# Windowed attention into a folded gated FFN on one core: first q, k loaded first and uncast, the weight fold by columns and then by rows, PSUM copies on either engine, a later believed DMA landing

## The chip, the cores and the metric

The kernel runs on one core of a Trainium2 chip. The metric is the device time of one execution in microseconds (us); the profile's span is about 2 us shorter. PE is the matmul engine, and PEld its weight load. DVE and ACT are the vector and scalar engines. POOL issues the loads that cast fp32 to bf16, and SP issues stores and DMA transposes. "Granted clock" (PEclk) is the share of full PE clock that the throttle grants. A run is called slow when it is over 1.5% above the fastest of the same kernel.

## The reference, cut to what matters

```python
# attention: q, k, v are (4, 8, 768, 64) fp32
scores = q @ k.T / 8          # keep the first 4 keys ("sink") and a causal window of 128
x = softmax(scores) @ v       # -> (3072, 512)
# feed-forward part
a = x @ w1; b = x @ w2        # 512 -> 1024 each
out = ((a * b) @ w3) @ w_out  # 1024 -> 1024 -> 512, fp32
```

Both kernels fold `w3 @ w_out` at the start into one 1024x512 matrix, `w3o`, so that the last two products become one for each token block. Four batches, 0 to 3, follow one another. Each has attention, "gate" products (with w1 and w2) and a "projection" (with w3o), in two halves of 384 tokens.

## The kernel before: the parts that matter

The program does not fix its instruction order by hand. It makes a list of operations with dependencies and modelled durations, and a list scheduler inside it picks, engine by engine, what it believes can start soonest. The order is frozen when the kernel is built.

```python
# POOL issues its casting loads in this order:
LOADS = """wo0 ident w3-1 wo1 w3-2 w3-3 wo2 k0-0-0 q0-0-0 tri k0-0-4 q0-0-4 w3-4 pick v0-0 v0-1 v0-2
    w3-5 w3-6 w3-7 w0 w1 k0-1-0 q0-1-0 v0-3 v0-4 v0-5 w2 w3
    b1-0 b1-1 b1-2 b1-3 b1-4 b1-5"""        # b1-n: k, q, v block n of batch 1
# (cut) batches 2 and 3: q, k are transposed by DMA from SP; the loads alternate k, q, v
for kb in range(NB):
    for s, n, src in ((0, "k", kN), (1, "q", qN)):
        got[n, b, kb] = load_nat(src, k if n == "k" else q, b, kb, fold_done)
        ...
        tp_of[s, kb] = Op(SP, TUS, dmt, [got[n, b, kb]] + war, base)
        tp_of[s, kb].turn = TUS
    got["v", b, kb] = load_v(b, kb)
# (cut) fold: one row block i of w3 at a time: 8 transposes, DVE copy, products, ACT copy
cpy = Op(DVE, dve_us(KFF * P, 2), lambda f=t3c, x=boxc: f(op=x), [a2], pr, frees=[(a, "mm")])
...
# (cut) x is transposed on PE for batches 0 and 1, by DMA for 2 and 3
if b < 2:
# (cut) what the scheduler picks on an engine: shortest wait, then priority
key = (0.0 if wait < 0.05 else wait, o.prio, o.serial)
# (cut) the landing belief
if hasattr(o, "turn"):                       # DMA transposes and stores
    busy = dma["at"] > start + 0.6
    dma["at"] = max(dma["at"], start + 0.6) + o.turn
    o.done = start + 0.6 + o.turn * (2 if busy else 1) + 1.3
if hasattr(o, "dma"):                        # loads
    dma["at"] = max(dma["at"], start + us + (0.1 if e == POOL else 0.6)) + o.dma
    o.done = dma["at"] + LAND
```

Two of PE's products are markers. `mm<-vN,sel` is the first that needs a batch's v, and only its first block ("v2-0" is that of batch 2). `mm<-qkT,ksbd`, the sink scores, is the first that needs a batch's transposed q and k.

The softmax here doesn't subtract the row's maximum and nothing guards it: scores larger than these inputs give would overflow.

## Time and profile before

| what | before | view |
|---|---|---|
| time | 215.36 us, median of 3 runs (214.5 to 229.22, the highest a slow run) | runs |
| span profiled, a fast run | 213.0 us | page |
| PE busy | 92% (DVE 51%, ACT 47%) | page, busy time |
| PE's longest wait | 4.9 us, before batch 2's sink scores | waits of PE |
| granted clock just after it | 0.57 | windows |

These lines are from the page of the kernel before. They are PE's line of busy time, three rows of the 40 equal slices of 5.3 us (busy share and granted clock in tenths), and the summary by engine of the chain that ended last.

```profile
PE 196.4 (92%) x1880; PEld 122.4 (57%) x1880; DVE 108.2 (51%) x249; ACT 100.1 (47%) x172; POOL 71.1 (33%) x93
PE   8899699969879999559999999999999999999994
PEclk9999999999999999958999999999999999999999
DMA  7999999999999999999999453210163030030033
PE 65%; DMA 25%; POOL 7%; issue 2%; ACT 0%; SPq 0%; POOLq 0%; ACTq 0%
```

PE is the only engine near its limit, and it is dense from slice 19 on. Whatever can be won lies in the first 100 us, where DMA is at 9 tenths. The dips of PE's row there are times in which the work in the frozen order waited for data.

The next lines are the waits of PE in the kernel before: engine, tile and line, what released it, total us, times, longest.

```profile
PE mm L427 <- DMA qkT<-big: 4.9, 1, 4.9
PE mm L407 <- DMA vN<-in_v_dram: 3.3, 3, 2.0
```

The next lines are from PE's timeline (start, us, instruction, count, and in brackets the idle time just before it with its releaser).

```profile
87.72 0.28 PE L538 MATMUL av<-vN,am 128*128 128x65 bf16 x4
92.91 0.62 PE L427 MATMUL mm<-qkT,ksbd 128*32 128x512 bf16 x4 [4.90 <-DMA qkT<-big]
```

The last one is the stretch after that wait in the windows view: stretch, us, then busy time of PE, PEld, DVE, ACT and POOL with counts, granted clock, DMA share, GB/s.

```profile
92.91:98.75 5.84, 5.84 (x35) 2.97 (x37) 2.26 (x4) 3.17 (x5) 1.64 (x2) 0.57 1.73 201
```

So the hole costs twice: 4.9 us idle, and then 5.8 us at little more than half speed. The last of batch 2's twelve DMA transposes of q, k landed at 92.66 us, by the trace's landing records, and PE went on at 92.91 us.

### The profile page before, as it was taken

The numbers are of one execution on the slowest core, as the hardware profiler recorded it, in microseconds if no ns is written. First come the engines' busy times: TensorE is split into PE (matmuls) and PEld (weight loads), VectorE is DVE, ScalarE is ACT, GpSimd is POOL, SyncE is SP. The second block draws the span as 40 slices with busy tenths as digits, with TensorE's granted clock in tenths as the row PEclk, the third lists the DMA queues.
The fourth block names the chain that finished last, engine by engine and source line by source line (L and its number), as shares of the span: only waits on it lengthen the run. The fifth ranks groups of instructions, "written<-read, shape, count | busy, mean of one in ns | idle before, by whom it ended". The sixth has DMA issues, their size and how long they took to land.

```text
span 213.0 us, 4649 instructions
## 1 busy us (share of the span) xinstructions
PE 196.4 (92%) x1880; PEld 122.4 (57%) x1880; DVE 108.2 (51%) x249; ACT 100.1 (47%) x172; POOL 71.1 (33%) x93
## 2 busy tenths in 40 slices
PE   8899699969879999559999999999999999999994
PEld 8797465536645665335665655566555556555542
DVE  3533766565986986316786444768504404314300
ACT  3135662757137772145874237786153243233232
POOL 7856763869999354732600000000000000000000
PEclk9999999999999999958999999999999999999999
DMA  7999999999999999999999453210163030030033
GB/s 140 181 194 184 199 196 177 192 160 155 151 147 131 120 144 131 155 238 131 155 153 118 116 133 83 94 51 3 34 182 82 0 148 0 3 148 0 2 148 148
DMA packets 98437, 26.25 MB, mean 123 GB/s; under 512 B 88944, under 2 KB 94320, under 8 KB 98416
## 3 DMA queue, kind: packets, MB, share of 16 engines
q0 software_dynamic: 74944, 14.42, 89.5%
q1 hardware_dynamic: 23472, 11.54, 25.9%
q8 instruction: 14, 0.23, 0.5%
q14 instruction: 7, 0.06, 0.1%
HBM read 29.36 MB, written 6.29 MB: 167 GB/s over the span
## 4 chain that ended last, share of the span: by engine, by line
PE 65%; DMA 25%; POOL 7%; issue 2%; ACT 0%; SPq 0%; POOLq 0%; ACTq 0%
PE mm L618 35%; PE mm L648 19%; DMA vN<-in_v_dram 8%; PE av L538 5%; DMA early<-in_k_dram 5%; DMA w_sb<-in_moe_w_dram 5%; PE sc L469 4%; DMA big<-in_moe_w_dram 4%; DMA qkT<-big 3%; POOL near L153 3%; POOL big L153 2%; POOL vN L153 1%; PE mm L574 1%; PE mm L427 1%; PE mm L407 0%
## 5 line engine op out<-in xcount | busy, mean ns | idle before, releaser
L618 PE MATMUL mm<-xT,w_sb 128*128 128x384 bf16 x512 | 91.6, 329 | 0.1
L618 PEld LDWEIGHTS <-w_sb 128*128 128x128 bf16 x512 | 48.0, 99 | 35.0 <-issue 4.4
L633 DVE TENSOR_TENSOR ab<-a_sb,mm 128x384 bf16<-128x384 f32 x64 | 35.3, 553 | 52.7 <-PE mm L618 48.2
L625 ACT COPY a_sb<-mm 128x384 f32<-128x384 f32 x64 | 30.6, 479 | 38.4 <-PE mm L618 21.9
L480 ACT ACTIVATE ex<-sc 128x768 bf16<-128x768 f32 (+2 forms) x52 | 44.1, 897 | 6.9 <-PE sc L469 6.7
L648 PE MATMUL mm<-w3o,ab 128*128 128x512 bf16 (+1 forms) x200 | 43.6, 370 | 0.0
L486 DVE TENSOR_TENSOR am<-ex,maskt 128x768 bf16<-128x768 bf16 (+2 forms) x52 | 30.0, 594 | 3.1 <-ACT ex L480 3.1
L648 PEld LDWEIGHTS <-ab 128*128 128x128 bf16 x200 | 19.3, 98 | 20.4 <-issue 0.2
L655 ACT COPY o_sb<-mm 128x512 f32<-128x512 f32 (+1 forms) x25 | 14.2, 568 | 34.6 <-PE mm L648 34.5
L153 POOL DMA_DIRECT2D vN<-in_v_dram x24 | 21.3, 888 | 11.6 <-DMA big<-in_k_dram 7.0
L538 PEld LDWEIGHTS <-am 128*128 128x128 bf16 x352 | 17.0, 97 | 3.2 <-issue 0.2
L538 PE MATMUL av<-vN,am 128*128 128x65 bf16 x352 | 18.8, 193 | 0.0
L553 DVE TENSOR_TENSOR xs<-av,rec 128x384 bf16<-128x384 f32 x32 | 17.7, 552 | 0.5
L300 PE MATMUL mm<-big,w3t 128*128 128x128 bf16 (+2 forms) x128 | 15.6, 273 | 0.1
L469 PE MATMUL sc<-qkT 64*128 64x256 bf16 (+1 forms) x248 | 14.6, 245 | 0.0
L304 ACT CAST w3o<-mm 128x128 bf16<-128x128 f32 (+2 forms) x16 | 6.0, 372 | 16.9 <-PE mm L300 16.8
L153 POOL DMA_DIRECT2D big<-in_q_dram x12 | 10.6, 882 | 6.7 <-DMA vN<-in_v_dram 6.6
L538 PE MATMUL av<-vsb,es 128*128 128x130 bf16 x64 | 12.8, 219 | 0.0
L153 POOL DMA_DIRECT2D big<-in_k_dram x12 | 10.5, 879 | 4.9 <-DMA big<-in_q_dram 3.1
L469 PEld LDWEIGHTS <-qkT 64*128 64x128 bf16 x248 | 8.2, 96 | 6.2 <-issue 5.2
L300 PEld LDWEIGHTS <-w3t 128*128 128x128 bf16 x128 | 9.5, 98 | 3.7 <-issue 0.4
L548 DVE RECIPROCAL rec<-av 128x6 f32<-128x6 f32 x32 | 6.2, 192 | 9.1 <-PE av L538 9.0
(52 smaller groups left out, 122.2 us busy)
## 6 DMA issues: line engine op xcount, KB each, us to landing
out_dram<-o_sb SPq DMA_DIRECT2D x23, 256.0 KB, 2.1
vN<-in_v_dram POOLq DMA_DIRECT2D x24, 128.0 KB, 9.9
w_sb<-in_moe_w_dram POOLq DMA_DIRECT2D x8, 256.0 KB, 9.8
big<-in_moe_w_dram POOLq DMA_DIRECT2D x7, 256.0 KB, 8.2
big<-in_k_dram POOLq DMA_DIRECT2D x12, 128.0 KB, 11.1
big<-in_q_dram POOLq DMA_DIRECT2D x12, 128.0 KB, 11.4
near<-in_k_dram POOLq DMA_DIRECT2D x6, 128.0 KB, 7.2
near<-in_q_dram POOLq DMA_DIRECT2D x6, 128.0 KB, 6.6
```

Source lines behind the costliest of these rows:

```text
L153: op = Op(eng, us, lambda: (nc.gpsimd if eng == POOL else nc.sync).dma_start(out=out, in_=in_), deps)
L300: nc.tensor.matmul(po, x[1].slot["w3t"][:, j, :], wo_sb[:, j, c0:c1], start=(j == 0), stop=(j == KFF - 1))
L469: nc.tensor.matmul(sc[:, e, c * P:(c + n) * P], T[hp, r, 0, kb * P:(kb + 1) * P], T[hp, r, 1, qb * P:(qb + n) * P], start=True, stop=True)
L480: nc.scalar.activation(y[1].slot["ex"][:, :, 0:w], y[0].slot["sc", i][:, :, 0:w], ACTF.Exp, scale=scale)
L486: nc.vector.tensor_mul(y[2].slot["am"][:, :, 0:w], y[1].slot["ex"][:, :, 0:w], maskt[:, :, m0:m0 + w].to_broadcast([P, 2, w]))
L538: nc.tensor.matmul(o, lhs, rhs, start=(i == 0), stop=(i == len(todo) - 1), skip_group_check=True)
L553: nc.vector.tensor_mul(xs_first[c].slot["xs"][:, :, r * P:(r + 1) * P].rearrange("p k (e d) -> p k e d", d=D), x[0].slot["av"][:, :, :, 0: ...
L618: nc.tensor.matmul(pg[:, 0:TOK], w_sb[:, kk, dt * P:(dt + 1) * P], holder[0].slot["xT"][:, kk, :], start=(kk == 0), stop=(kk == NP - 1))
L625: nc.scalar.copy(y[1].slot["a"][:], y[0].slot["mm"][:, 0:TOK])
L633: nc.vector.tensor_mul(abh[0].slot["ab"][:, dt, :], y[1].slot["a"][:], y[2].slot["mm"][:, 0:TOK])
L648: nc.tensor.matmul(x[0].slot["mm"][:, 0:n1 - n0], abh[0].slot["ab"][:, kk, mi * P:(mi + 1) * P], w3o[:, kk, n0:n1], start=(kk == 0), stop= ...
L655: nc.scalar.copy(x[1].slot["o"][:, n0:n1], x[0].slot["mm"][:, 0:n1 - n0])
```

## The change

Its intent is to let PE start on attention sooner, to keep PE, DVE and ACT fed by placing copies on whichever is free, and to reorder loads. Its parts:

1. Batch 0's first q, k are loaded as fp32 by SP and ACT, and cast on DVE and ACT.
2. POOL's loads are reordered: batch 0's first v ahead of the fold's weights, all gate weights (`w0`..`w3`) ahead of the second half of batch 0, and the q, k loads of batches 2 and 3 ahead of all v loads of the same batch.
3. The fold handles the first three row blocks of w3 by columns into three held PSUM banks, the other five by rows.
4. Nine kinds of PSUM copies may go to ACT or DVE (`EITHER`), as the scheduler sees fit.
5. Batch 2's x is transposed on PE, not by DMA.
6. The landing belief changes: a transpose is done when the modelled DMA queue reaches it, not at most two turns after its issue; and each casting load is believed to take 2% longer.

Some smaller edits go with these: the projection's products are queued in halves of four, some set-up work is split, and the model's starting values differ.

```diff
-    LOADS = """wo0 ident w3-1 wo1 w3-2 w3-3 wo2 k0-0-0 q0-0-0 tri k0-0-4 q0-0-4 w3-4 pick v0-0 v0-1 v0-2
-        w3-5 w3-6 w3-7 w0 w1 k0-1-0 q0-1-0 v0-3 v0-4 v0-5 w2 w3
-        b1-0 b1-1 b1-2 b1-3 b1-4 b1-5"""
+    for r in range(2):
+        for n, src in enumerate((k, q)):
+            # (cut) fp32 into a home that is free until later
+            def first(r=r, n=n, src=src, i=i):
+                (nc.scalar if n else nc.sync).dma_start(out=first_home[i][...], in_=src[0, ...])
+    LOADS = """ident k0-0-4 q0-0-4 tri v0-0 pick v0-1 v0-2 w3j-0-1 wo-0-1 w3j-1-2 wo-1-2 w3j-2-4 wo-2-4
+        w3j-4-6 wo-4-6 w3j-6-8 wo-6-8 w3-3 w3-4 w3-5 w3-6 w3-7 w0 w1 w2 w3 k0-1-0 q0-1-0 v0-3 v0-4
+        v0-5 k1-0 q1-0 v1-0 (cut) k2-0 q2-0 k2-1 q2-1 k2-2 q2-2 k2-3 q2-3 k2-4 q2-4 k2-5 q2-5 v2-0 v2-1
+        v2-2 v2-3 v2-4 v2-5 (cut: batch 3 likewise)"""
@@ fold (cut)
+    for j in range(KFF):          # columns of the first KA = 3 row blocks
+        cpy = Op(EITHER, (act_us(KA * P), dve_us(KA * P, 2)), t3c, [a], ...)
+        last = Op(PE, cols(DM, KA), fm, ..., takes=["sc", "mm"] if j == 0 else [], ...)
@@ copies
-                ac = Op(ACT, act_us(TOK), acopy, [g1], 0, takes=["a"], frees=[(g1, "mm")])
+                ac = Op(EITHER, (act_us(TOK), dve_us(TOK)), acopy, [g1], 0, takes=["a"], frees=[(g1, "mm")])
@@ x transposed
-            if b < 2:
+            if b < 3:
@@ landing belief
             if hasattr(o, "turn"):
-                busy = dma["at"] > start + 0.6
                 dma["at"] = max(dma["at"], start + 0.6) + o.turn
-                o.done = start + 0.6 + o.turn * (2 if busy else 1) + 1.3
+                o.done = dma["at"] + 1.3
-            if hasattr(o, "dma"):
-                dma["at"] = max(dma["at"], start + us + (0.1 if e == POOL else 0.6)) + o.dma
+            if hasattr(o, "dma") and e == POOL:
+                dma["at"] = max(dma["at"], start + us + 0.1) + o.dma * 1.02
```

## The prediction

> **What bounds the kernel now.** The page's PE 92% busy counts waits inside matmul records. I price PE's work at the pace of dense stretches of the chain of waits (0.65 us for four 128x384 gate matmuls, 1.73 us for eight 128x512 projection matmuls), times the counts of the instruction order: about 183 of the 213.0 us span. The other 30 us, by how far PE lags behind its work (timeline of PE):
> - 13 us at 36 us (second q, k half of batch 0), 20 us at 64 us: starved by loads. The chain has 25% DMA. The last first-layer weight lands at 45.1 us, batch 1's last q at 60.3, batch 2's first v at 63.9 (PE waits for both).
> - Batch 2's twelve DMA transposes (issued 62.2 to 87.1 us) leave PE idle 4.9 us up to 92.9 us. The granted clock is then 0.57 over 92.9 to 98.8 us: about 2 us more. The Trainium skill, "TensorE: Matmul & The Clock Gate", Part 1, says an idle window of about 3.4 us halves the clock; this trace agrees.
> - Then PE is dense to 210 us; the last copy and store take 3 us.
>
> **What the change does.** PE work hardly changes: the fold keeps 64 transposes, its products become 64 of 128x512 (13.8 us; before 14 us in narrower pieces). Batch 2's xT moves from DMA to PE (24 transposes, +1.3 us). Sum: 184 us. Bytes stay. First q, k on the SP and ACT queues share the same 16 DMA engines (the skill, "DMA: Bandwidth & Descriptors", "Issuing engines are not separate DMA queues"): they win order, not bandwidth. Order changes:
> - The fold's 6 MB come after batch 0's first q, k, v; all first-layer weights before the second q, k, v half. When that lands (about 42 us, at 350 GB/s: 14.7 MB read by 45 us), 30 us of PE work stand before it in the instruction order, against 23.
> - 79 us, against 68, stand before batch 2's first scores; its q, k loads come before its v.
>
> **Where that leads.** PE lag: 9 us when the column fold's last load lands (20 us), 10 to 12 at the last gate weight, then set by batch 1's loads, still behind the same bytes: its second half lands near 60 us, with 46 us of work before it instead of 41: lag 14, not 19. Batch 2's scores are wanted near 93.5 us, ready by 80 to 92: no hole, no cold clock. 184 + 14.5 + 1.5 small stalls + 3 tail = 203 us span, plus 2.4 us from span to median time: 205.4 us.
>
> **Critical path.** About 5 us from the early order, 7 us from hole and clock, less 1.3 and small stalls. First start and engine choice (both half idle): under 2 us.
>
> **What would show it.** PE's wait on DMA qkT before batch 2's sink scores under 1.5 us; granted clock near 1.0; gate and projection lines over 58% of the chain (now 54%), DMA under 18%.
>
> **What would make it wrong.** The order is fixed from modelled times: one late load stalls everything behind it. One score bank is held during the column fold: batch 0's scores may stall. Batch 0's stores queue behind twelve transposes on SP. Then 208 to 212. If batch 1's loads come earlier: 199.
>
> 205.4 us, 8 in 10 between 200 and 211; faster by over 2%: 0.87, within 2%: 0.11, slower: 0.02.

## The result and the profile after

The changed kernel took 206.06 us in the median of 4 runs (205.12 to 211.06), against 214.93 us (214.1 to 229.22, a slow run; the other three are at most 215.36). Two more runs of the changed kernel took 206.16 and 209.72 us (slow). The ratio is 0.959, with a 95% interval of 0.9536 to 0.9644. Here and below a ratio is the mean time of one kernel's fast runs over that of the other's of the same rounds, so it is not quite the ratio of the medians.

The first profile of the changed kernel fell in a slow run (211.06 us, span 209.3). The same file was therefore run again, unedited (experiment E1), and its profile is of a fast run (206.54 us, span 204.8). That one is "the profile after" below; the slow one stands beside it where it shows something. These lines are from the page after, fast, and answer to those of before.

```profile
PE 193.1 (94%) x1778; PEld 115.8 (57%) x1778; DVE 106.5 (52%) x247; ACT 108.5 (53%) x176; POOL 73.0 (36%) x96
PE   7659999999999998999999999999999999999993
PEclk9976999999999999999999999999999999999998
DMA  6999999999999999999999933000145120030034
PE 44%; DMA 39%; POOL 12%; issue 2%; ACT 0%; DVE 0%; ACTq 0%; POOLq 0%
```

The dips of PE's row at slices 5, 9, 11 to 12 and 17 to 18 are gone. A new dip stands in slices 1 to 3, with a lower clock in slices 3 and 4, and a small one in slice 16. The page's chain now has *more* DMA than before in a faster run; this is taken up below.

The waits of PE after:

```profile
PE mm L320 <- DMA big<-in_moe_w_dram: 2.1, 3, 1.4
PE mm L461 <- DMA vN<-in_v_dram: 1.4, 3, 1.0
```

There is no wait for transposed q, k any more. The timeline shows PE passing the marker of batch 2 (last line) without idling, and a short wait for batch 2's v before it.

```profile
79.10 0.82 PE L675 MATMUL mm<-xT,w_sb 128*128 128x384 bf16 x4
80.88 0.39 PE L461 MATMUL mm<-vN,sel 128*128 128x512 bf16 x1 [0.95 <-DMA vN<-in_v_dram]
90.82 5.36 PE L675 MATMUL mm<-xT,w_sb 128*128 128x384 bf16 x32
96.11 0.40 PE L481 MATMUL mm<-qkT,ksbd 128*32 128x512 bf16 x4
```

The early stretch in the windows view, after, has the columns as above:

```profile
9.60:13.00 3.40, 1.84 (x25) 1.07 (x25) 2.68 (x7) 2.62 (x7) 3.40 (x5) 0.91 1.46 174
13.00:20.00 7.00, 5.65 (x47) 3.39 (x45) 3.22 (x9) 2.99 (x7) 3.89 (x8) 0.56 1.27 192
```

PE is busy 1.84 of 3.40 us, in small pieces, and the next 7 us run at 0.56 of full clock. In this kernel, the first 20 us are worse than before.

One reason stands in the code of both kernels. Up to 24 us, the scheduler puts zero matmuls into PE's modelled waits, but only as long as its first score bank has never been used. The kernel before got 96 of them, the last at 19.0 us, and its clock was 1.00 from 9.60 to 13.00 us, with PE busy 3.32 of 3.40 us. The changed kernel starts batch 0's scores at 7.0 us and got 34, the last at 6.7 us.

The next table sums where PE's time went in the traces. Each matmul is given the interval that its shape takes in dense stretches (162 ns for 384 columns, 216 for 512, 109 for 256, 56 for 128, 30 for 65; half of that where two share the array and start 3 ns apart, a quarter where four do). What the start of the next one is later than that is "lost"; the zero matmuls that only keep the clock up count as lost, and so does the first 1.1 us. The three traces hold all matmul records.

| us | before | after, fast | E4 below |
|---|---|---|---|
| work at dense pace | 175.6 | 176.8 | 175.6 |
| lost, 0 to 20 us | 10.4 | 14.0 | 12.7 |
| lost, 20 to 70 us | 12.5 | 4.2 | 6.3 |
| lost, 70 to 100 us | 8.6 | 2.8 | 9.6 |
| lost, 100 us to the last matmul | 2.6 | 3.3 | 2.6 |
| last matmul to end of span | 3.3 | 3.7 | 3.3 |

So the span's 8.2 us (213.0 to 204.8) are 4.7 us from the first 70 us, and 5.8 us from the hole of batch 2 with its cold clock, less 1.2 us of extra work and 1.1 us of small items at the end.

### The profile page after: what moved, and what is told of

Its sections match the earlier page's. It is cut to its first block, busy times and chain, and to the rows that moved or that the text cites. A ratio compares the mean times of both kernels' runs of the same rounds, so it can differ in the third digit from the quotient of the medians.

```text
span 209.3 us, 4424 instructions
## 1 busy us (share of the span) xinstructions
PE 196.5 (94%) x1763; PEld 118.4 (57%) x1778; DVE 107.1 (51%) x247; ACT 108.6 (52%) x176; POOL 73.0 (35%) x96
## 4 chain that ended last, share of the span: by engine, by line
PE 77%; DMA 11%; POOL 5%; ACT 2%; DVE 2%; issue 1%; ACTq 0%
PE mm L675 36%; PE mm L705 18%; DMA vN<-in_v_dram 8%; PE av L595 6%; PE mm L358 4%; PE sc L524 4%; DMA big<-in_moe_w_dram 3%; POOL big L157 2%; PE sc L328 2%; PE mm L631 2%; POOL vN L157 1%; PE mm L328 1%; PE mm L351 1%; DMA out_dram<-o_sb 1%; PE mm L320 1%
## 5 line engine op out<-in xcount | busy, mean ns | idle before, releaser
L705 PE MATMUL mm<-w3o,ab 128*128 128x512 bf16 (+1 forms) x189 | 44.7, 374 | 1.2 <-issue 0.4
L140 ACT COPY a_sb<-mm 128x384 f32<-128x384 f32 x56 | 26.9, 480 | 35.2 <-PE mm L675 17.7
L140 ACT COPY o_sb<-mm 128x512 f32<-128x512 f32 (+1 forms) x24 | 13.6, 569 | 33.4 <-PE mm L705 30.6
L595 PE MATMUL av<-vN,am 128*128 128x65 bf16 x352 | 19.9, 198 | 0.0
L595 PEld LDWEIGHTS <-am 128*128 128x128 bf16 x352 | 18.0, 101 | 2.6 <-DVE am L543 0.3
L524 PE MATMUL sc<-qkT 64*128 64x256 bf16 (+1 forms) x248 | 15.2, 247 | 0.9 <-ACT ex L537 0.7
L595 PE MATMUL av<-vsb,es 128*128 128x130 bf16 x64 | 13.3, 226 | 0.0
L140 ACT COPY qkT<-mm 128x384 bf16<-128x384 bf16 (+1 forms) x15 | 8.1, 594 | 2.3 <-PE mm L428 1.3
L358 PE MATMUL mm<-big,w3t 128*128 128x512 bf16 x38 | 9.0, 379 | 0.1
L140 ACT COPY w3t<-mm 128x384 bf16<-128x384 bf16 (+1 forms) x9 | 5.8, 660 | 6.1 <-PE mm L320 5.5
```

The costliest lines, as they stand in the source:

```text
L140: (nc.scalar.copy if turn_of[0] == ACT else nc.vector.tensor_copy)(out, in_)
L358: nc.tensor.matmul(x[2].slot["mm"][:], x[1].slot["w3t"][:, j, :], wo_sb[:, j, :], start=(j == 0), stop=(j == KFF - 1))
L524: nc.tensor.matmul(sc[:, e, c * P:(c + n) * P], T[hp, r, 0, kb * P:(kb + 1) * P], T[hp, r, 1, qb * P:(qb + n) * P], start=True, stop=True)
L595: nc.tensor.matmul(o, lhs, rhs, start=(i == 0), stop=(i == len(todo) - 1), skip_group_check=True)
L705: nc.tensor.matmul(x[0].slot["mm"][:, 0:n1 - n0], abh[0].slot["ab"][:, kk, mi * P:(mi + 1) * P], w3o[:, kk, n0:n1], start=(kk == 0), stop= ...
```

## The experiments

The theory: the gain is in the order. One share comes from the loads' new order (early), and the other from the later believed landing, which puts more PE work ahead of batch 2's sink scores. Engine choice, column fold and uncast loads carry little. The rival: engine choice and fold carry it, by keeping PE from waiting on copies. A second question came out of the slow profile: "q, k before v" makes v2-0 late and opens a new hole. All runs gave right results. Each group shared one chip and the runs of the kernel before; the kernel before took 214.38 us in the first group (E1 to E4), 215.03 in the second (E5 to E8) and 214.54 in the third (E9 to E12), in the median. One run of each experiment was profiled.

### E1: the changed kernel again, unedited

> The changed kernel itself, unedited, for a profile in the fast state (the first one fell in the slow state, 209.3 us of span). Theory: about 205 to 206.5 us; PE's lost time (start-to-start gaps of matmuls above the dense pace) about 25 us against 33 before; the idle of about 3.5 us before the wait for batch 2's first v is there again at about 80 us, with a cold clock after it; the half clock between 14 and 21 us that the slow profile showed is shorter or absent. If the slow profile was typical, the same 30 us are lost and the half clock is there.

Measured: 206.77 us (206.02 to 211.13, 4 runs), ratio 0.9634 (0.9598 to 0.967). One of the four was slow, at 211.13 us, like the first profile. The expectation missed twice: the wait for batch 2's v is 0.95 us and not 3.5, and the half clock is there (13 to 20 us, above). The first profile, the slow one, has this line in its timeline of PE, at the place where the fast one waits 0.95 us:

```profile
83.40 0.61 PE L461 MATMUL mm<-vN,sel 128*128 128x512 bf16 x1 [3.31 <-DMA vN<-in_v_dram]
```

And this is its windows view just after it:

```profile
84.00:90.00 6.00, 5.78 (x45) 3.75 (x44) 4.13 (x10) 0.00 (x0) 3.38 (x4) 0.58 1.84 155
```

The chain of waits shows when this v was issued by POOL and how long it took to land (start, us), first in the fast profile and then in the slow one:

```profile
68.78 12.05 DMA vN<-in_v_dram
```

```profile
67.31 16.04 DMA vN<-in_v_dram
```

It follows that the changed kernel traded the hole before batch 2's q, k for a new one before batch 2's v. It is small when the 128 KB land in 12 us and 3.3 us when they take 16, and then the clock falls too. What follows tests this on fast runs.

### E2: batch 2's first v before its twelve q, k loads

```diff
+    late_names = [("k", 2, kb) if s == 0 else ("q", 2, kb) for kb in range(NB) for s in range(2)] + [("v", 2, 0)]
+    slots = [got[n] for n in late_names]
+    fns = [o.fn for o in slots]
+    for o, f in zip(slots, fns[-1:] + fns[:-1]):
+        o.fn = f
```

The scheduler's slots stay as they were and only what they issue is rotated. So the order on PE, DVE, ACT and SP is the same and one load moves.

> Only the first v load of batch 2 is issued before that batch's twelve q, k loads instead of after them; the order on every other engine is identical. Theory (the hole near 80 us is only this load landing late, 16 us after its issue, behind q, k loads and DMA transposes): the 3.5 us idle and the cold clock after it go, 200 to 202.5 us. Rival (the DMA engines are simply full there, so something of batch 2 is late whatever comes first): PE waits for batch 2's transposed q, k instead, 204.5 us or more.

Measured: 205.79 us (204.96 to 207.67), ratio 0.9587 (0.9549 to 0.9625), none slow. The interval overlaps that of E1, and the expected 200 to 202.5 us were missed. The profile, at 207.67 us the slowest of the four, had no wait on batch 2's v, nor on its transposed q, k as the rival said, but one of 2.2 us on batch 3's first v. Moving one v cures one hole, and in this run the next one of the same kind appears.

### E3: each free copy pinned to the engine that it had before

```diff
-        cpy = Op(EITHER, (act_us(KA * P), dve_us(KA * P, 2)), t3c, [a], 50 + j, takes=["w3t"], frees=[(a, "mm")])
+        cpy = Op(DVE, dve_us(KA * P, 2), t3c, [a], 50 + j, takes=["w3t"], frees=[(a, "mm")])
 # (cut) likewise for the other EITHER copies; the scheduler then made another order
```

> Every PSUM copy is put back on the one engine it had in the kernel before (w3t and xT on DVE, fold results, a and o on ACT, batch 0's q, k by turns, batch 1's on DVE); the rest of the change stays. Theory (loads and order set the pace, DVE and ACT are half idle): within 1.5 us of the changed kernel, 204.5 to 207.5 us. Rival (the free choice of engine carries the gain by returning PSUM buffers sooner): 209 us or more.

Measured: 210.09 us (209.67 to 210.72), ratio 0.9803 (0.977 to 0.9837). That is about half of the gain gone, which is what the rival said. But the scheduler had made another order (of PE's 1744 weight loads, zero ones left out, 1040 differ from the changed kernel's at the same place), so this run changes two things at once. E5 and E10 separate them.

### E4: the kernel before with only the new order of loads

```diff
-    LOADS = """wo0 ident w3-1 wo1 w3-2 w3-3 wo2 k0-0-0 q0-0-0 tri k0-0-4 q0-0-4 w3-4 pick v0-0 v0-1 v0-2
-        w3-5 w3-6 w3-7 w0 w1 k0-1-0 q0-1-0 v0-3 v0-4 v0-5 w2 w3
+    LOADS = """ident k0-0-0 q0-0-0 k0-0-4 q0-0-4 tri v0-0 pick v0-1 v0-2 wo0 w3-1 wo1 w3-2 w3-3 wo2 w3-4
+        w3-5 w3-6 w3-7 w0 w1 w2 w3 k0-1-0 q0-1-0 v0-3 v0-4 v0-5
```

> The kernel before with one edit: its load list in the new order (batch 0's first q, k, v, then the fold, then all first-layer weights, then the second q, k, v half), still by casting loads, row fold and pinned copies. Theory (order is what frees PE early, but batch 2's transposed q, k still arrive near 92 us, so part of it is given back as a longer hole): 210 to 213 us; PE's lost time between 20 and 80 us falls from 13 to 9 us or less, the idle before batch 2's sink scores grows from 5 to 7 us or more. Rival (the order brings nothing without the uncast first loads and the column fold): 214 us or more.

Measured: 212.14 us (210.96 to 213.57), ratio 0.9899 (0.9846 to 0.9953). The lost time of 20 to 70 us fell from 12.5 to 6.3 us (table above), most of what the whole change won there. But PE came to batch 2's marker with 71 us of work in front of it, not the 79 of the changed kernel, so the hole grew. (These are counts of the instruction order. The matmuls in front of the marker in the traces, zero ones left out, sum to 64 us before, 68 in E4 and 75 in the changed kernel.) This is its line among the waits of PE:

```profile
PE mm L427 <- DMA qkT<-big: 6.2, 1, 6.2
```

A faster beginning, alone, runs PE into the same late DMA. The early gain is given back at the hole.

### E5: copies pinned, with the order frozen as in the changed kernel

```diff
+    def pin(op, eng):
+        op.pinned = eng
+        return op
 # (cut) each EITHER copy wrapped: pin(Op(EITHER, ...), DVE) or pin(..., ACT)
-            turn_of[0] = e
+            turn_of[0] = getattr(o, "pinned", e)
```

The scheduler still believes in its own choice; only the engine that gets the instruction changes. The order on PE, SP and POOL is the same as in the changed kernel; on PE, all 1778 weight loads of the traces agree.

> As e3 (every PSUM copy on the engine of the kernel before), but the schedule is not made anew: PE, SP and POOL keep the changed kernel's order exactly, and each copy stands on its old engine at its place in that order. e3 cost about 3.3 us against the changed kernel. Theory A (where the copies run matters by itself: one engine gets a queue of copies while PE waits for the PSUM buffer): 208.5 us or more again. Theory B (e3 lost its time because the scheduler, with pinned copies, made another order, in which ACT stands 9 us in front of the fold's results): below 207.8 us, within 1 us of the changed kernel.

Measured: 209.32 us in the median of 4 (209.36, 209.28, 206.55, and a slow 211.12), ratio 0.9667 (0.9605 to 0.9728). This is inconclusive: its profile has the wait for v2-0 at 3.3 us, so the late v stands in the runs and hides the copies. E10 repeats it without the late v.

### E6: batch 2's loads in the order k, q, v again

```diff
+    late6 = [got[n] for kb in range(NB) for n in (("k", 2, kb), ("q", 2, kb))] + [got["v", 2, kb] for kb in range(NB)]
+    fns = [got[n, 2, kb].fn for kb in range(NB) for n in "kqv"]
+    for o, f in zip(late6, fns):
+        o.fn = f
```

> Batch 2's v loads are put back between its q, k loads, as in the kernel before; the order on PE, ACT, DVE and SP is the changed kernel's. Theory (the hole before batch 2 closed because more PE work now stands before it: PE comes there at 95 us, and even the old load order has q, k ready by about 93): within 1 us of the changed kernel, wait on the transposed q, k under 1.5 us; the wait for batch 2's first v gone. Rival (it closed because q, k are loaded ahead of v): idle of 3 us or more before batch 2's sink scores, 209 us or more.

Measured: 204.61 us (204.5 to 206.12), ratio 0.9529 (0.9495 to 0.9563). It is the changed kernel with one of its own edits undone for batch 2, and it is at least as fast. This is the marker of batch 2 in its timeline:

```profile
94.37 0.40 PE L486 MATMUL mm<-qkT,ksbd 128*32 128x512 bf16 x4 [0.41 <-issue]
```

With v loads between them, q and k are only just late. The view names no DMA for the idle 0.41 us, but by the landing records the last of the twelve transposes landed at 94.28 us, 0.09 us before PE went on, so this wait is for them. In the changed kernel (E1) they landed at 90.95 us, 5 us before PE came. So "q, k before v" was not what filled most of the hole of 4.9 us, since undoing it opens 0.41 us again. It was not needed for the time here, and it made the new hole.

### E7: dummy matmuls in PE's early waits

```diff
+        n_pe, FILL = 0, {4: 8, 6: 4, 9: 14, 10: 6, 13: 9, 17: 24}
+            if e == PE:
+                for i in range(FILL.get(n_pe, 0)):
+                    to = o.slot["mm"] if n_pe >= 10 else av_home[0]
+                    nc.tensor.matmul(to[:, 0:P], zeros[:], zeros[:], start=True, stop=True)
+                n_pe += 1
```

This puts 65 zero products into the sparse stretch of 7 to 16 us, to keep the clock up.

> The changed kernel with 65 dummy matmuls on zeros put into PE's early waits (7 to 14 us), order otherwise identical. In the fast profile of the changed kernel the granted clock was half from 13.1 to 19.9 us and PE lost 5.3 us between 10 and 20 us. Theory (the early waits drop the clock, and the work in 13 to 20 us then runs at half pace): clock stays 1.0, 1.5 to 2.5 us faster, 204 to 205 us. Rival (PE only waits for loads there, so a full clock just waits longer): no gain, or 0.5 us lost to the dummies.

Measured: 208.53 us (207.36 to 210.08, 6 runs), ratio 0.9703 (0.9664 to 0.9742): slower than the changed kernel, a miss. The dummies did their work: the granted clock of 13 to 20 us was 1.00. But PE then came to v2-0 0.95 us earlier than in E1 (78.98 us), the v landed 0.8 us later, and the wait was longer. These are the two lines of its timeline and of its windows view.

```profile
81.63 0.39 PE L461 MATMUL mm<-vN,sel 128*128 128x512 bf16 x1 [2.65 <-DMA vN<-in_v_dram]
```

```profile
82.00:86.50 4.50, 4.28 (x42) 2.81 (x41) 3.36 (x8) 0.00 (x0) 1.83 (x3) 0.62 1.74 157
```

A wait of 2.65 us in a fast run is followed by a stretch at 0.62 of the clock. What was won early was lost at the late v, with interest; E8 tests this.

### E8: E7 with the first v of batches 2 and 3 before the q, k of its batch

```diff
+    for vb in (2, 3):
+        slots = [got["kq"[s], vb, kb] for kb in range(NB) for s in range(2)] + [got["v", vb, 0]]
+        fns = [o.fn for o in slots]
+        for o, f in zip(slots, fns[-1:] + fns[:-1]):
+            o.fn = f
```

> e7 and, for batches 2 and 3, the first v load issued before the twelve q, k loads; other engines' order identical. e2 moved batch 2's only, gained about 1 us, and PE then waited 2.35 us for batch 3's first v at 111.5 us. Theory: both waits gone, 2 to 3.5 us under the changed kernel, 203 to 204.5 us. Rival (as in e2 the wait moves on, to the transposed q, k): no better than e7.

Measured: 204.64 us (203.96 to 205.52, 6 runs), ratio 0.9517 (0.9489 to 0.9544), the lowest ratio; E6, on the same chip, is level with it. The time is just above the 203 to 204.5 us expected. Against E7, on the same chip and in the same rounds, two loads that moved are worth about 4 us. PE no longer waits for the first v of batch 2 or of batch 3 (0.2 us on batch 1's are left). This is the early stretch in the windows view, where the changed kernel had 0.56:

```profile
13.00:20.00 7.00, 6.72 (x93) 4.87 (x94) 3.48 (x11) 4.22 (x8) 4.00 (x8) 1.00 1.24 184
```

### E9 and E10: the two v loads moved without dummies, then with copies pinned

E9 is the changed kernel with the edit of E8 alone; E10 is E9 with the edit of E5.

> The changed kernel with batch 2's and batch 3's first v load each issued before the twelve q, k loads of its batch; nothing else moved, no dummies. In e8 (with dummies) this gave 204.6 us, with dummies alone e7 gave 208.5. Theory: the late v is what costs, the dummies hardly matter: 203.9 to 205.5 us, and no runs above 208 us (the slow runs of the changed kernel are those whose wait for this v is long enough to halve the clock). Rival: dummies and v order are both needed: 206 us or more.

> e9 with every PSUM copy on the engine of the kernel before, order of PE, SP and POOL as in e9. It tells what e5 left open, because e5's runs split (206.6 to 211.1 us) on the wait for batch 2's first v. Theory (in a fixed order the engine of a copy hardly matters; e3 lost by the other order that the scheduler then made): within 1 us of e9. Rival (placement itself gives the 3 us): 2 us or more above e9.

Measured: E9 205.19 us (203.78 to 206.65, 6 runs), ratio 0.9568 (0.9531 to 0.9605). E10 205.05 us (204.52 to 206.28, 6 runs), ratio 0.9568 (0.9543 to 0.9593). Pinning every copy to its old engine changed nothing that the intervals could show (0.3 to 0.4% each way), once the order was held and the late v was away. So the choice of engine as such carries no more of the gain than that. What E3 lost came from the other order that the scheduler made with fewer choices. Which wait of that order costs the 3 us I did not find. ACT idling before the fold's results, which I suspected first, was there in E10 too (one wait of 11.2 us) and cost nothing.

### E11: the kernel before with two of the six parts

```diff
 # on top of E4
-                busy = dma["at"] > start + 0.6
                 dma["at"] = max(dma["at"], start + 0.6) + o.turn
-                o.done = start + 0.6 + o.turn * (2 if busy else 1) + 1.3
+                o.done = dma["at"] + 1.3
-                dma["at"] = max(dma["at"], start + us + (0.1 if e == POOL else 0.6)) + o.dma
+                dma["at"] = max(dma["at"], start + us + (0.1 if e == POOL else 0.6)) + o.dma * 1.02
```

This keeps the row fold, the fixed engines, the casting first loads and the DMA transposes of batch 2's x. It has the new landing belief and the early part of the new load order, as E4 has it, and nothing else; batches 2 and 3 still load k, q, v in turn.

> e4 (the kernel before with the new load order) and the changed kernel's rule for when a DMA transpose or a casting load is done in the scheduler's reckoning; no uncast first loads, no column fold, copies pinned, xT of batch 2 by DMA. The scheduler then puts about 80 us of PE work ahead of batch 2's scores, against 71 in e4. Theory (load order and this later reckoned landing together are the gain): 206 to 209 us, idle before batch 2's sink scores under 2 us (6.4 in e4). Rival (column fold, first loads or free engines are needed): 210.5 us or more.

Measured: 205.75 us (205.18 to 207.96, 6 runs), ratio 0.9624 (0.9582 to 0.9665), against 0.9634 and 0.959 for the whole change, and just below the 206 to 209 us expected. These two parts together reproduce the whole gain; the order alone, in E4, is worth 1%. The belief alone was not run. The old rule believed a transpose done at most two turns after its own issue, however many were queued before it. The new rule lets it wait for the queue, so the scheduler expects batch 2's q, k later. By the count in its instruction order, PE has 80 us of work in front of batch 2's marker, where E4 has 71. PE passes the marker without idling:

```profile
100.65 0.40 PE L427 MATMUL mm<-qkT,ksbd 128*32 128x512 bf16 x4
```

The last transpose had landed at 92.97 us. PE came this late in part because of a wait before it: this profile is of one of the two slower runs (207.92 and 207.96 us), and it has the known cause at another place, batch 3's first v. POOL issued it at 80.07 us, and PE wanted it before it had landed. These are the line of POOL's timeline and that of PE's:

```profile
80.07 0.88 POOL L153 DMA_DIRECT2D vN<-in_v_dram  x1 [1.18 <-DMA big<-in_k_dram]
```

```profile
92.16 0.57 PE L407 MATMUL mm<-vN,sel 128*128 128x512 bf16 x1 [2.63 <-DMA vN<-in_v_dram]
```

### E12: E7 with k, q, v in turn for batches 2 and 3

```diff
+    for vb in (2, 3):
+        slots = [got[n, vb, kb] for kb in range(NB) for n in "kq"] + [got["v", vb, kb] for kb in range(NB)]
+        fns = [got[n, vb, kb].fn for kb in range(NB) for n in "kqv"]
+        for o, f in zip(slots, fns):
+            o.fn = f
```

> An attempt at the fastest: the changed kernel with v loads between q, k loads for batches 2 and 3 and the dummies of e7. e6 (batch 2 only, no dummies) gave 204.6. Theory: 203 to 205 us, if batch 3's q, k are not late; if they are, PE waits before batch 3's sink scores near 125 us and the time is 206 us or more.

Measured: 205.42 us (204.91 to 205.72, 4 runs), ratio 0.9578 (0.9558 to 0.9597). It is not better than E8, and it missed the 203 to 205 us expected, at batch 2 and not at batch 3:

```profile
95.52 0.40 PE L487 MATMUL mm<-qkT,ksbd 128*32 128x512 bf16 x4 [1.47 <-issue]
```

The view names no releaser, but the last of batch 2's transposes landed at 95.42 us, 0.1 us before PE went on. So this is again the wait for transposed q, k, and here "q, k before v" would have been of use.

### All of them

| kernel | median us | ratio to before | 95% |
|---|---|---|---|
| changed kernel, first | 206.06 | 0.959 | 0.9536 to 0.9644 |
| E1 changed kernel again | 206.77 | 0.9634 | 0.9598 to 0.967 |
| E2 v2-0 first | 205.79 | 0.9587 | 0.9549 to 0.9625 |
| E3 copies pinned, new order | 210.09 | 0.9803 | 0.977 to 0.9837 |
| E4 before + load order | 212.14 | 0.9899 | 0.9846 to 0.9953 |
| E5 copies pinned, order held | 209.32 | 0.9667 | 0.9605 to 0.9728 |
| E6 batch 2's v between | 204.61 | 0.9529 | 0.9495 to 0.9563 |
| E7 dummies | 208.53 | 0.9703 | 0.9664 to 0.9742 |
| E8 dummies + first v first | 204.64 | 0.9517 | 0.9489 to 0.9544 |
| E9 first v first | 205.19 | 0.9568 | 0.9531 to 0.9605 |
| E10 E9 + copies pinned | 205.05 | 0.9568 | 0.9543 to 0.9593 |
| E11 before + order + belief | 205.75 | 0.9624 | 0.9582 to 0.9665 |
| E12 dummies + v between | 205.42 | 0.9578 | 0.9558 to 0.9597 |

E8 has the lowest ratio: about 5% below the kernel before, and about 1% below the changed kernel (0.9517 against 0.9634 and 0.959, ratios of different groups; the interval touches that of the first measurement at its edge). The kernels without the late v (E6, E8, E9, E10, E12) stayed at or below 206.65 us in all of their 26 runs. The changed kernel itself had 3 of 10 runs at 209.7 us or more.

Left open: the column fold, the uncast first loads and the transposes of batch 2's x on PE were not tried one by one. E11 lacks all three and its interval overlaps that of the changed kernel, so no gain of theirs shows; one of 1 us or so is not excluded. The new belief with the old order of loads was not run, so the share of each is known only in one order: 1% for the loads alone, the rest when the belief is added. The two halves of the belief (the transposes' rule and the factor 1.02) were not separated. E11 with the two v loads moved was not run.

## Why the prediction was right or wrong

It said 205.4 us and the runs gave 206.06. The mechanism that it named, more PE work in front of late loads, is the one that the runs show. That the number came so close is in part luck: the spans of the fast runs were 203.4 to 204.7 us, where it had 203, but the step from span to time was 1.7 us, where it had 2.4; and inside the early gain a larger win and an unforeseen loss happen to sum to the size predicted. Point by point:

- **"About 5 us from the early order"**: the lost time of 0 to 70 us fell by 4.7 us (22.9 to 18.2). The size is right but its make-up is not: 20 to 70 us gave 8.3 us, and the first 20 us cost 3.6 us that the prediction did not have.
- **"7 us from hole and clock"**: 70 to 100 us gave 5.8 us. The wait for transposed q, k was to be under 1.5 us, and it is gone. PE came to batch 2's marker at 96.11 us, predicted near 93.5. Of the 1.2 us missing, the new wait for v2-0 holds 0.95 us in the fast profile.
- **PE work +1.3 us**: the sum at dense pace rose by 1.2 us. The prediction's level (183 us before) is higher than the 175.6 us of the sum, which counts the 96 zero matmuls (5.4 us at that pace) as lost.
- **"Engine choice ... under 2 us"**: E10 against E9 shows none in a held order. The scheduler's other order without the choice (E3) costs 3 us more, so the choice matters to what the scheduler makes, not to the engines' load.
- **"They win order, not bandwidth"** for the first q, k on SP and ACT: by the Trainium skill, "DMA: Bandwidth & Descriptors", section "Issuing engines are not separate DMA queues", DMAs of all issuing engines run on the same 16 DMA engines. This agrees as far as it goes: over the first 20 us the DMA engines moved 175 GB/s with these loads and 176 before (windows view). PE's first transposes of q, k began at 4.54 us with them and at 6.98 us in E4 without them. No gain in time shows for that: E11 without these loads took 205.75 us, the changed kernel 206.06.
- **Mostly wrong: "its q, k loads come before its v"**, given as a reason why there would be no hole. E6 undid it and was no slower; PE then waited 0.41 us (1.47 us in E12) for q, k, against 4.9 us before. So the work in front of the marker filled most of the hole, and this edit only the rest. The edit's larger effect was the late v, which the prediction did not see: it asked of each load whether it came earlier, and not which load came later for it.
- **Wrong: "granted clock near 1.0"**. It is 0.56 over 13 to 20 us in the fast profile, where PE had its work in small pieces and no zero matmuls between them. Putting 65 in (E7 and E8) brought it to 1.00. In E8 that is worth little more than E9 without it (0.9517 against 0.9568).
- **Wrong test: "gate and projection lines over 58% of the chain, DMA under 18%"**. The fast profile has 38% (24% and 14%) and DMA 39%, with the kernel faster. The slow profile of the same kernel has 54% and DMA 11%. The chain follows the release that came last, and a load that lands just after it is wanted takes the chain over to DMA for its whole 12 us of flight, at a cost of 1 us or less. As a test of an order change it says the opposite of the truth here.
- **"One late load stalls everything behind it"**, named as what would make it wrong: that is what the profiles of a slow run and of E7 show.

## What to carry to other kernels

Where a scheduler freezes the order from modelled landing times, look first at what it believes about late DMAs: a later believed landing puts work in front of the late batch, and here that and the load order together gave the whole 4%, without the new fold and the free choice of engines. A small load that is wanted first must not stand behind the bulk of its group; move that one load, and check who came later for it. Where a view names no releaser of a wait, look up when the awaited transfers landed. Count a PE wait near 3 us twice, once for the wait and once for the clock after it (here, where PE was otherwise dense, waits of 2.6 us and more were followed by a lower clock, and those of 2.05 and 2.19 us were not), and judge an order change by PE's waits and its lost time, not by the shares of the chain of waits.

## What the Trainium skill lacked or had wrong

- "TensorE: Matmul & The Clock Gate", section "HAM oscillation", gives the rule of no PE idle gap over about 3.4 us. Before, 4.9 us idle were followed by 0.57 of the clock, which agrees. But E7's gap of 2.65 us was followed by 0.62 over 82.0 to 86.5 us, and E11's of 2.63 us by 0.72 over 92.5 to 98.0 us, so the rule is too generous here, as is the "~3µs" of the page's section "Why this matters for your kernels". Gaps of 2.05 us (before, at 47.89 us) and 2.19 us (E2, at 114.04 us) were followed by 1.00.
- The same page describes short idle times that lower the clock without a long gap, but lacks a figure for how sparse the work must be. Here, 1.84 us of PE work in 3.40 us (9.6 to 13.0 us, after) were followed by 0.56 over the next 7 us, and 65 zero products in the gaps brought it to 1.00 (E7, E8); 2.15 us in the same stretch of E4 were followed by 1.00.
- The same page, section "Back-to-back issue gap", gives 131 ns as the sustained interval of matmuls with 512 columns and says that the formula for a single one (216 ns) over-counts. Dense stretches here ran at 216 ns (ten projection matmuls, from 186.78 to 188.94 us of the profile before), and at 162 ns for 384 columns (64 gate matmuls, from 188.94 to 199.34 us), which is the formula and not the sustained figure.
- "DMA: Bandwidth & Descriptors", section "Anatomy of one DMA — SWDGE (gpsimd) path", fits one load as 2.0 us plus its bytes over 436 GB/s, which is 2.3 us for 128 KB by that formula. The page says that DMAs interleave on the engines, but gives no time for a load behind others: the v loads of 128 KB took 9.9 us from issue to landing in the median before, and v2-0 took 12.05 and 16.04 us in two profiles of one kernel. A schedule is made of such landings, and these two profiles are of runs of 206.54 and 211.06 us.
